# A gated mix of a long convolution and a GEGLU block on one core: loads from two queues, last rows in four groups, a half tile of the down product in row halves, part of the final mix on ScalarE and GpSimd

## The chip, the core and the metric

The kernel runs on one core of a Trainium2 chip. A core has TensorE (PE in the profile; its weight loads are PEld), VectorE (DVE), ScalarE (ACT), GpSimd (POOL) and SyncE (SP), and 16 DMA engines that move data between DRAM and the on-chip memory. SP issues DMAs in order from its queue, and so can ACT from its own. Matrix products land in eight accumulation banks that DVE and ACT must empty ("evacuate") before they can be used again. The metric is the device time of one execution in microseconds (us), as the median of several; a lower time is better.

## The reference

The input is a sequence `x` of 2048 positions with 640 channels. The output mixes two branches with one gate value for each position:

```python
g = sigmoid((x * gate_w).sum(-1, keepdims=True))
a = conv(x, K) + x * Dskip          # K[d, l] = Re(sum_n C[d,n] * exp(dt*A[d,n]*l) * dt*B[d,n]), by FFT
b = (gelu(x @ w_gate) * (x @ w_up)) @ w_down
return g * a + (1 - g) * b
```

The convolution is causal and as long as the sequence; its kernel `K` is made from complex parameters `A`, `B`, `C` with 128 states for each channel. The inner width of `b` is 1728, that is 13 tiles of 128 and one half tile of 64.

## The kernel before

**The work.** The convolution is a product of spectra. The transforms are matrix products with sine tables, in two stages: stage A works across 16 "phases" (positions modulo 16) and its result goes through a DRAM buffer (`dU` for the input, `dKA` for the kernel K) so that stage B finds other rows together. K itself is built for half of the channels at a time (`kgen`, L736): exponentials on ACT (L647, L675), phases on DVE (L624 to L628), sines on ACT (L633), their products on DVE (L661, L662, L685), a contraction with 640 small matmuls for both halves (L711), a selection (L722), a store to `dS` (L731), and 18 gathers out of `dS` (L804, L812) that feed stage A (L840). A spectrum and its copy with swapped rows (L881) are multiplied with K's spectrum (L888). The inverse stage B (L899) works in eight chunks `c`; each chunk is evacuated by ACT or DVE (L259, L263) and stored to `dY` (L907). `finish` (L910) loads from `dY` into eight tiles (L913), does the last stage with `WAT` for 16 phases (L922) and mixes each phase on DVE (L927): `z = psum * g + z`, where `z` already holds `(1 - g) * b`. Two stores for each pair of phases bring it out (L931).

**The block b.** For two halves of the sequence, `gate` (L536) and `up` (L557) multiply into pairs of banks; ACT applies gelu (L548), DVE multiplies (L568). The last weight tile holds the 64 gate columns and the 64 up columns side by side, so for tile 13 the up half is read from the upper 64 rows of the bank (L552). `downs` (L584) makes 16 tiles of the down product, each from 28 matmuls: 14 tiles of the inner width (tile 13 with zeros in its lower half, set by GpSimd at L486 and L531) times two column halves.

**The order of the work.** Every step is an entry of a `Plan`: which engines may do it, what it reads and writes, a cost and a rank. A planner's result, the list `ORDER` (952 numbers), is written into the kernel: each number names a step, its engine and its bank pair, and `emit` (L130) issues the steps in exactly this order. The costs (`mm`, `dma`, the numbers in `ve(...)`, `pool(...)`) therefore issue nothing; they are the planner's input only. Each engine works through its own steps in the order of the list. All DMAs are issued by SP, one after the other, and a DMA that waits holds those behind it.

**Names used later.** `ldtT` is log_dt, `prT` the parameters A to C, `xT` four transposed tiles of x (640 KB each), `Wg`, `Wu` and `Wd` weight tiles, `un` and `ua` one phase of x and its stage A, `kst` and `kst2` the contraction's results, `last_rows` (L400) the one-column fields from which `WAT`'s phases (L949 to L952) are made, `z` or `zt` the output tiles.

Of the kernel before, what the change touches and what calls it, by code (L numbers as in the profile page):

```python
# [27 lines left out]
    12 336 6316 316 536 436 516 396 1432 24 376 692 676 988 416 496 476 456 356 616 1004 576 636 1564 556 44 1628  # L28
    656 736 936 596 1064 816 756 2740 1608 64 956 776 716 836 876 1104 1588 796 916 1044 976 2861 1024 896 2836 84
    856 1648 1664 2982 2956 2768 1084 4383 1724 3076 3008 104 2780 2888 1164 1688 4404 1124 1442 1501 2856 2903 1144  # L30
    2804 1748 1784 2976 3020 2924 128 3096 1208 1464 6323 9384 6362 1496 1524 6436 1704 3341 1556 4428 1188 1228
    6388 6348 3436 3222 3044 3368 6416 1764 3103 3316 3248 1808 3380 3196 4444 1844 6441 3456 3262 6468 3404 1868
    1824 6481 3336 3700 6556 6508 3128 6536 1244 3461 3796 3284 3728 144 3143 3556 3488 1884 1268 6562 3216 6600
    3581 6676 6588 6628 1284 168 6656 1304 3822 3676 1324 1344 3608 3500 3916 3848 6721 3576 6748 6682 6796 1364
    6708 4181 3524 6776 1388 3164 3942 4276 4208 1404 2124 6840 4036 6803 3968 3861 6916 6868 2184 6828 2008 3622
    6896 3936 1904 3740 3696 2088 2024 3884 1928 6963 3816 3764 6921 6988 7036 2104 2048 3980 3644 6948 2064 1968
    4063 7016 1944 4056 4004 2148 4222 1984 4156 184 7081 264 4296 7040 2208 7156 2244 7108 7068 4301 2224 288 7136
    208 4088 224 4376 4244 7200 4328 7163 7224 4102 7276 7188 4344 248 7256 2164 4176 4124 2268 7280 2304 7323 4501
    7396 7348 7308 2284 7376 2328 2364 4702 4528 9484 2388 7443 7400 2344 4661 7516 7428 7468 2404 9508 7496 9544
    4728 2420 4688 9604 7523 2444 7562 7548 2461 7636 7588 7616 2503 2484 7640 2524 7682 7668 2541 7756 7708 4580  # L40
    2564 9408 7736 7803 9468 4604 7762 4461 7876 7784 7824 9524 9448 7856 2580 2622 9788 4743 4484 2644 9428 9804
    2604 9828 2716 7881 4764 7922 2676 4620 7996 7904 7948 2736 2696 9844 9908 7976 9748 9924 8556 4543 4644 9868
    8436 8376 9764 8236 8456 9568 9884 8576 8516 8536 8416 8256 8041 4564 8476 8002 4900 8496 8024 8116 8068 8316
    9664 9628 8296 8096 5023 8396 4996 8336 9584 8276 4928 8356 4782 5116 5048 9644 8121 4876 4808 8160 5063 8148
    8188 9688 9944 8216 5382 5136 5141 5476 5084 9968 9704 8620 5236 8583 8608 8648 4823 10064 5408 8676 4940 4896
    5168 4844 10004 8682 5016 8721 8708 5423 8748 8776 4964 10028 5182 5496 5444 9984 5261 5256 5204 10088 8820
    10124 5356 8783 5742 8808 8848 5503 5288 10184 5836 8876 5620 5768 5596 9724 11236 5528 11016 10044 8921 5648
    5716 5302 8948 10104 10148 8883 5324 5376 5540 8904 8976 5781 5564 5616 10208 10164 11322 11283 5856 11020 11348
    11304 11048 8982 5804 9023 9008 5660 9048 10224 9076 11142 11456 10241 5684 11168 5736 11243 11362 10264 10360
    11268 11388 9083 10384 9121 9108 11582 9144 11460 11608 11103 11484 11061 9176 11128 11542 11676 11564 11500  # L50
    11088 10323 12116 11524 9182 10344 9221 9208 10280 9248 9276 11682 11803 10304 11656 11721 11708 11416 11748
    11216 12242 11824 11196 12200 12268 12121 11636 12224 9283 11436 12148 9322 11896 9304 9348 10400 10441 10424
    9376 12163 11762 10468 12184 6080 11788 10536 10496 11856 10516 11876 5861 6108 12316 12296 10556 5983 5956 5888
    12616 12756 6122 6008 6076 11900 11941 6144 11983 11928 11968 12020 12004 5902 12476 12048 12336 13176 13216
    13256 13236 6161 5924 13336 13436 13196 13376 5976 12663 12620 6188 6242 12684 13296 13516 12644 13416 13356
    12724 13276 12343 13496 12481 6268 12704 12520 12096 13316 12364 12508 13396 13456 6284 12548 12383 6201 13476
    12408 12896 12584 13036 12076 12424 13620 12444 13522 13648 13563 13544 13588 12800 12828 12564 13723 13616
    13662 13748 6224 12760 14556 13688 12943 12964 12788 13081 13716 13042 13108 13064 12900 13763 14336 12928 13821
    13124 13862 13788 6020 12984 13888 13816 13144 13848 13004 13916 13963 10892 14642 6044 13921 13988 13948 14683
    14664 14560 14708 14601 14016 14584 14916 14462 14628 14343 14776 14484 14368 14020 14061 14048 10904 14123  # L60
    14382 14148 14084 14160 14188 14263 14404 14116 14221 14288 15180 14216 14244 14962 14756 15208 15263 14736
    14984 14921 15288 14316 15500 14944 14422 15528 10643 14444 10928 12844 14536 14516 12864 10952 15004 14781
# [978 lines left out]
```

## Time and profile before

| quantity | value |
|---|---|
| median of 3 runs | 312.56 us (311.97 to 314.31) |
| profiled execution: time, span | 310.86 us, 309.1 us |
| PE busy | 260.2 us (84%), 2446 matmuls |
| PEld busy | 142.4 us (46%) |
| DVE busy | 246.8 us (80%), 373 instructions |
| ACT busy | 221.8 us (72%), 274 instructions |
| POOL busy | 5.2 us (2%), 17 instructions |
| DMA | 60.62 MB, queue busy 60.6% of 16 engines |
| chain that ended last | PE 41%, DVE 12%, DMA 11%, SP's queue 8%, ACT 5% of the span |

The span runs from the first to the last recorded instruction of one profiled execution; the execution's own time has a little more around it. A busy share is an average over the whole span, and the stages have different limits. PE's busy time is modelled: matmuls overlap, so a busy PE is not PE at its peak. A group's row gives its line, engine, operation, the form (partitions x elements, type), the count, the busy time, the mean time of one in ns, and the engine's idle time ahead of it with what ended most of that. Instructions of one engine overlap a little, so the distance between two starts can be less than the mean duration. The chain of waits is followed back from the last instruction; "issue" in it is time in which the engine waited for nothing that the profile shows, and SPq is the DMA issue on SP's queue.

### The profile page before, as it was taken

The numbers are of one execution on the slowest core, as the hardware profiler recorded it, in microseconds if no ns is written. First come the engines' busy times: TensorE is split into PE (matmuls) and PEld (weight loads), VectorE is DVE, ScalarE is ACT, GpSimd is POOL, SyncE is SP. The second block draws the span as 40 slices with busy tenths as digits, with TensorE's granted clock in tenths as the row PEclk, the third lists the DMA queues.
The fourth block names the chain that finished last, engine by engine and source line by source line (L and its number), as shares of the span: only waits on it lengthen the run. The fifth ranks groups of instructions, "written<-read, shape, count | busy, mean of one in ns | idle before, by whom it ended". The sixth has DMA issues, their size and how long they took to land.

```text
span 309.1 us, 6162 instructions
## 1 busy us (share of the span) xinstructions
PE 260.2 (84%) x2446; PEld 142.4 (46%) x2446; DVE 246.8 (80%) x373; ACT 221.8 (72%) x274; POOL 5.2 (2%) x17
## 2 busy tenths in 40 slices
PE   0699899899599799997899986998677999999471
PEld 0253344344257676743444455443233656666230
DVE  4999999999999849689999874526768799993494
ACT  3999999999998689999898952853558845640000
POOL 4000000000000000000000000000001100000000
PEclk9999999999799999999999997799959999999975
DMA  6995344444231321645336567996597976789886
GB/s 205 391 296 168 106 140 133 127 127 129 85 127 67 108 78 54 186 139 155 106 113 200 200 194 257 334 348 193 168 335 272 333 220 193 279 266 343 254 245 171
DMA packets 45859, 60.62 MB, mean 196 GB/s; under 512 B 4803, under 2 KB 38150, under 8 KB 45830
## 3 DMA queue, kind: packets, MB, share of 16 engines
q1 hardware_dynamic: 45830, 60.23, 60.6%
q8 instruction: 19, 0.31, 0.4%
q14 instruction: 10, 0.08, 0.1%
HBM read 35.80 MB, written 19.17 MB: 178 GB/s over the span
## 4 chain that ended last, share of the span: by engine, by line
PE 41%; DVE 12%; DMA 11%; SPq 8%; ACT 5%; issue 4%; DVEq 0%; ACTq 0%
PE ps L592 12%; PE ps L544 10%; PE ps L564 8%; SPq L804 4%; DMA arena<-dU 4%; ACT arena L259 3%; PE ps L711 3%; DMA dY<-arena 3%; DVE arena L685 3%; DVE arena L927 3%; DVE arena L568 2%; PE ps L867 2%; PE ps L899 2%; SPq L913 2%; DVE arena L263 2%
## 5 line engine op out<-in xcount | busy, mean ns | idle before, releaser
L259 ACT CAST arena<-ps 128x640 bf16<-128x640 f32 (+1 forms) x110 | 70.5, 696 | 34.9 <-PE ps L867 11.0
L544 PE MATMUL ps<-arena 128*128 128x512 bf16 x280 | 67.0, 397 | 15.8 <-DMA arena<-in_w_gu_dram 11.0
L592 PE MATMUL ps<-arena 128*128 128x320 bf16 x448 | 63.2, 299 | 0.0
L564 PE MATMUL ps<-arena 128*128 128x512 bf16 x260 | 60.4, 384 | 2.1 <-ACT arena L259 0.8
L263 DVE CAST arena<-ps 128x640 bf16<-128x640 f32 (+3 forms) x62 | 50.4, 847 | 14.5 <-PE ps L711 6.9
L544 PEld LDWEIGHTS <-arena 128*128 128x128 bf16 x280 | 28.1, 101 | 51.5 <-issue 11.5
L592 PEld LDWEIGHTS <-arena 128*128 128x128 bf16 x448 | 43.0, 98 | 18.2 <-issue 0.8
L633 ACT ACTIVATE arena<-arena 128x2560 bf16<-128x2560 int16 x18 | 41.6, 2334 | 1.3 <-DVE arena L628 0.9
L568 DVE TENSOR_TENSOR arena<-ps,arena 128x1024 bf16<-128x1024 f32 x26 | 31.5, 1219 | 13.2 <-PE ps L564 13.1
L564 PEld LDWEIGHTS <-arena 128*128 128x128 bf16 x260 | 25.4, 99 | 32.4 <-issue 4.4
L548 ACT ACTIVATE arena<-ps 128x1024 bf16<-128x1024 f32 (+1 forms) x28 | 27.2, 1022 | 8.8 <-PE ps L544 8.5
L888 DVE TENSOR_TENSOR arena<-arena 128x1280 bf16<-128x1280 bf16 x32 | 24.5, 818 | 2.2 <-DMA arena<-arena 1.9
L867 PE MATMUL ps<-arena 64*64 64x320 bf16 x256 | 18.1, 334 | 7.0 <-DMA arena<-dKA 1.8
L647 ACT ACTIVATE arena<-arena 128x640 bf16<-128x640 f32 x32 | 21.0, 745 | 1.3 <-DVE arena L737 1.2
L265 DVE TENSOR_SCALAR arena<-ps,omg 128x640 bf16<-128x640 f32 x10 | 8.8, 881 | 11.0 <-PE ps L592 11.0
L626 DVE SCALAR_TENSOR_TENSOR arena<-arena 128x320 int32<-128x320 f32 x40 | 16.9, 484 | 0.0
L867 PEld LDWEIGHTS <-arena 64*64 64x64 bf16 x256 | 8.7, 110 | 16.9 <-issue 10.7
L675 ACT ACTIVATE arena<-arena 128x320 bf16<-128x320 f32 x40 | 16.3, 511 | 0.0
L927 DVE SCALAR_TENSOR_TENSOR arena<-ps,g_f,arena 128x640 bf16<-128x640 f32 x16 | 13.1, 877 | 3.6 <-PE ps L922 3.5
L711 PE MATMUL ps<-arena 128*64 128x40 bf16 x640 | 12.3, 189 | 4.2 <-issue 3.7
L840 PE MATMUL ps<-arena 128*128 128x320 bf16 x64 | 13.0, 326 | 3.1 <-DMA arena<-dS 2.1
L628 DVE TENSOR_SCALAR arena<-arena 128x1280 int32<-128x1280 int32 x18 | 14.9, 827 | 0.6
(105 smaller groups left out, 227.9 us busy)
## 6 DMA issues: line engine op xcount, KB each, us to landing
arena<-in_w_gu_dram SPq DMA_DIRECT2D x52, 160.0 KB, 2.3
dU<-arena SPq DMA_DIRECT2D x16, 320.0 KB, 2.3
dKA<-arena SPq DMA_DIRECT2D x16, 320.0 KB, 4.0
arena<-dU SPq DMA_DIRECT2D x8, 640.0 KB, 4.7
arena<-arena SPq DMA_DIRECT2D x16, 320.0 KB, 3.6
arena<-dKA SPq DMA_DIRECT2D x16, 320.0 KB, 4.0
dY<-arena SPq DMA_DIRECT2D x8, 640.0 KB, 5.5
arena<-in_u_nat_dram SPq DMA_DIRECT2D x16, 160.0 KB, 2.3
```

Source lines behind the costliest of these rows:

```text
L259: nc.scalar.copy(out=dst, in_=src(b))
L263: nc.vector.tensor_copy(out=dst, in_=src(b))
L544: nc.tensor.matmul(ps[:, k + j, :], lhsT=Wg[w][:, kt, :], rhs=xT[2 * grp + j][:, kt, :], start=(kt == 0), stop=(kt == NKT - 1))
L548: add({"ACT": an(1024) + 60}, lambda s: nc.scalar.activation(out=HTall[0:p, :, f, :], in_=ps[0:p, plan.bank(g):plan.bank(g) + 2, :], func= ...
L564: nc.tensor.matmul(ps[:, k + j, :], lhsT=Wu[w][:, kt, :], rhs=xT[2 * grp + j][:, kt, :], start=(kt == 0), stop=(kt == NKT - 1))
L568: add({"DVE": v1(1024)}, lambda s: nc.vector.tensor_tensor(out=HTall[:, :, f, :], in0=ps[:, plan.bank(u):plan.bank(u) + 2, :], in1=HTall[: ...
L592: nc.tensor.matmul(ps[:, k + h, 0:W], lhsT=HTq[q][:, f, 128 * j:128 * j + 128], rhs=Wd[f][:, W * h:W * h + W], start=(f == 0), stop=(f == ...
L633: ac(an(8 * W) + 90, lambda: nc.scalar.activation(out=t[:], in_=ph.bitcast(I16)[:, :, :, 0:16:2], func=ACT.Sin, scale=SIN_SCALE), r=[f"ph{ ...
L711: nc.tensor.matmul(ps[64 * y:64 * y + 64, k + i // g, 40 * (i % g):40 * (i % g) + 40], lhsT=cs1[:, x, 80 * y + k0 + i, :], rhs=cs2[:, x, 8 ...
L867: nc.tensor.matmul(ps[64 * y:64 * y + 64, k + x, 0:W], lhsT=TB[64 * x:64 * x + 64, m, :], rhs=t[64 * x:64 * x + 64, 2 * a + y, HV[h]], sta ...
L888: ve(v2(W * CS), lambda x=x: nc.vector.tensor_tensor(out=x[:, :, HV[h]], in0=x[:, :, HV[h]], in1=t, op=ALU.mult), r=ks, w=[k for k in kx i ...
L927: add({"DVE": v1(D)}, lambda s, p=p, ph=ph, z=z: nc.vector.scalar_tensor_tensor(out=z, in0=ps[:, plan.bank(p):plan.bank(p) + 2, 0:W], scal ...
```

## The change

- `dma` gets an argument `q`, the queues from which a transfer may be issued; ACT's queue is allowed for some. In the new list ACT issues the loads of log_dt, A_re and A_im, two loads of the last rows and six of the 16 output stores. All others stay on SP.
- The eight chunks of `dY` are put into four groups of rows in place of three (chunks 0 to 3, 4 and 5, 6, 7), and a load of the last rows covers one, two or four tiles in place of one: 12 loads in place of 24. `last_rows` is changed to fit the new row order and moves from DVE to GpSimd, where it is 18 one-column instructions.
- The half tile 13 is copied by a DMA from the lower to the upper 64 rows (`HTall[0:FL]` to `HTall[FL:128]`), its weights are loaded into both row halves, and the two memsets go. In `downs` the last matmul of each column half uses 64 rows, one half each.
- In the final mix, phases 1, 4, 7 and 10 go another way: ACT writes `psum * g` in fp32 to one of three buffers, and GpSimd adds it to `z`.
- The planner's costs are changed (for example `mm` from n / 2.28 + 4 to n / 2.36 + 4), and `ORDER` is new as a whole (945 numbers).

```diff
-    def dma(kb, fn, r=(), w=(), rank=5.0, run=1280, **k):
-        return add({"SP": 450}, lambda s: fn(), r, w, rank=rank, lat=1900, x=max(100, kb * (3.7 if run < 1000 else 3.3 if run < 2500 else 2.9)), **k)
+    def dma(kb, fn, r=(), w=(), rank=5.0, run=1280, q=("SP",), **k):
+        def go(s):
+            queue[0] = nc.scalar if s["eng"] == "ACT" else nc.sync
+            fn()
+
+        return add({e: 450 for e in q}, go, r, w, rank=rank, lat=1900, x=max(100, kb * (3.3 if run < 1000 else 2.8 if run < 2500 else 2.7)), **k)
...
     def last_rows():
...
+        v = nc.gpsimd
+        s_, hi, lo = sc8[:, 6:7], sc8[:, 9:10], sc8[:, 10:11]
+        x, y = sc8[:, 12:13], sc8[:, 14:15]
+        v.tensor_scalar(out=x, in0=B2, scalar1=4.0, scalar2=P5, op0=ALU.mult, op1=ALU.add)
...
+        for out, p7, p1, p0 in ((s_, x, y, P3), (hi, B4, B3, B2), (lo, B3, B2, B1)):
+            select(v, y, B1, p7, p1, 13)
+            select(v, out, B0, y, p0, 13)
...
-    ve(2000, last_rows, r=["fld"], w=["lrow"], rank=P["T2"])
+    pool(5000, last_rows, r=["fld"], w=["lrow"], rank=P["T2"])
...
+    dma(160, lambda: queue[0].dma_start(out=ldtT[:], in_=A_log_dt.partition_broadcast(N)), w=["ldtT"], rank=0, q=("ACT",))
...
+        dma(80, lambda: queue[0].dma_start(out=Wd[NFF][FL:128, :], in_=B_w_down[128 * NFF:128 * NFF + FL, :]), w=[(f"Wd{NFF}", 1)], rank=rank)
...
+            dma(128, lambda: queue[0].dma_start(out=HTall[FL:128, :, f, :], in_=HTall[0:FL, :, f, :]), r=HK(f), w=[(f"HT{q}", "z") for q in range(2)],
+                rank=RMUL, run=640)
...
                 for h in range(2):
-                    for f in range(NFT):
+                    for f in range(NFF):
                         nc.tensor.matmul(ps[:, k + h, 0:W], lhsT=HTq[q][:, f, 128 * j:128 * j + 128], rhs=Wd[f][:, W * h:W * h + W],
-                                         start=(f == 0), stop=(f == NFT - 1))
...
+                                         start=(f == 0), stop=False)
+                for h in range(2):
+                    nc.tensor.matmul(ps[:, k + h, 0:W], lhsT=HTq[q][FL * h:FL * h + FL, NFF, 128 * j:128 * j + 128],
+                                     rhs=Wd[NFF][FL * h:FL * h + FL, W * h:W * h + W], start=False, stop=True)
...
-        for q, (p0, st, cs) in enumerate(((0, 2, (0, 1, 2, 3)), (1, 4, (4, 5)), (3, 4, (6, 7)))):
-            for g, (t, nm) in enumerate(tiles):
...
+        rows = ((0, 2, (0, 1, 2, 3), (2, 2, 2, 2)), (1, 4, (4, 5), (4, 4)), (3, 8, (6,), (4, 4)), (7, 8, (7,), (1, 1, 2, 4)))
+        for q, (p0, st, cs, gs) in enumerate(rows):
+            g = 0
+            for n in gs:
+                dst = wide[g // 4][p0:128:st, 4 * (g % 4):4 * (g % 4 + n), :]
...
+                    q=("SP", "ACT") if q == 3 else ("SP",))
+                g += n
...
+                if ph not in POOLED:
+                    add({"DVE": 880}, lambda s, p=p, ph=ph, z=z: nc.vector.scalar_tensor_tensor(
+                        out=z, in0=ps[:, plan.bank(p):plan.bank(p) + 2, 0:W], scalar=g_f[:, ph:ph + 1], in1=z, op0=ALU.mult, op1=ALU.add),
+                        r=["g"], w=[(f"zt{ph // 8}", ph % 8)], frees=p, rank=R)
+                    continue
+                y, yn = tmp[POOLED.index(ph) % len(tmp)]
+                add({"ACT": 800}, lambda s, p=p, ph=ph, y=y: nc.scalar.activation(
+                    out=y.rearrange("p (h w) -> p h w", h=2), in_=ps[:, plan.bank(p):plan.bank(p) + 2, 0:W], func=ACT.Copy, scale=g_f[:, ph:ph + 1]),
+                    r=["g"], w=[yn], frees=p, rank=R)
+                pool(1700, lambda ph=ph, y=y: nc.gpsimd.tensor_tensor(
+                    out=zt[ph // 8][:, ph % 8, :], in0=y, in1=zt[ph // 8][:, ph % 8, :], op=ALU.add), r=[yn], w=[(f"zt{ph // 8}", ph % 8)], rank=R)
...
+                    r=[(f"zt{g // 4}", 2 * (g % 4) + b) for b in range(2)], rank=R, run=2560, q=("SP", "ACT"))
```

In the new list, the order of the steps that the prediction speaks of is this. SP begins with one `un`, xT0, Wg0, xT1, the second half of the last down weight tile and Wg1. The four stores to the second half's `dS` are adjacent on SP, and between its first and last gather stand nine other transfers: a store to `dKA`, two row swaps, four loads of K chunks, a weight load and the second copy of half tile 13. After the last inverse matmuls PE does three down tiles (before: two), then the last rows of phases 13, 14, 9, 15, 12, 4, 3, 5, 1, 2, 7, 6, 0, 8, 10, 11. ACT does the mixes of phases 4, 1, 7 and 10 in this order with its output stores between them, and GpSimd its adds in the same order. The last output stores, of phases 10 and 11, are issued one on each queue.

## The prediction

> **What bounds the kernel now.** I read the page's totals first, then the busy time by stretch, then the end of the chain of waits with the timeline beside it, then groups and transfers. The profiled execution took 310.86 us (span 309.1 us, 1.76 us around it); the median of the three runs is 312.56 us, 1.7 us more. Busy time by stretch (length; busy us and instructions of PE, PEld, DVE, ACT, POOL; granted clock; DMA share; GB/s); 175.4 is the end of the last sine of the kernel generation, 282.9 the point where only two down products are left besides the last rows:
>
> ```profile
> 0.00:175.40 175.40, 153.09 (x1174) 80.95 (x1174) 154.95 (x260) 161.80 (x187) 3.13 (x15) 0.99 0.47 151
> 175.40:282.90 107.50, 94.20 (x1182) 54.31 (x1179) 77.05 (x96) 60.04 (x89) 2.09 (x2) 0.94 0.79 262
> 282.90:309.10 26.20, 12.91 (x96) 7.19 (x94) 14.84 (x18) 0.00 (x0) 0.00 (x0) 0.74 0.79 232
> ```
>
> So there are three limits. In the first stretch ACT is busy 161.8 of 175.4 us, DVE and PE close behind: a balance of three. In the second PE is busy 94.2 of 107.5 and DMA 79%. In the third ACT and POOL do nothing, and DVE works 14.8 of 26.2 us. From the timeline (start, length, engine, line, count, idle before):
>
> ```profile
> 279.41 7.78 PE L592 MATMUL ps<-arena 128*128 128x320 bf16 x56
> ...
> 284.28 10.02 SPq L913 DMA_DIRECT2D arena<-dY  x16
> ...
> 290.32 0.73 PE L922 MATMUL ps<-arena 128*64 128x320 bf16 x8 [3.13 <-DMA arena<-dY]
> 290.90 3.28 DVE L927 SCALAR_TENSOR_TENSOR arena<-ps,g_f,arena 128x640 bf16<-128x640 f32 x4 [2.79 <-PE ps L922]
> ...
> 294.39 11.56 SPq L931 DMA_DIRECT2D out_dram<-arena  x16
> 294.91 9.87 DVE L927 SCALAR_TENSOR_TENSOR arena<-ps,g_f,arena 128x640 bf16<-128x640 f32 x12 [0.73 <-PE ps L922]
> ```
>
> The last inverse ends on PE at 279.4. Two down tiles hide the way of its result through DRAM until 287.2; then PE idles 3.1 us. SP issues 16 loads at 0.6 us each, so the loads come one by one, and afterwards 16 mixes on DVE set the end. The chain says the same:
>
> ```profile
> 275.49 8.77 DMA dY<-arena
> ...
> 289.25 0.59 SPq L913
> 289.84 0.04 issue
> 289.88 3.13 DMA arena<-dY
> ```
>
> The rows for prices, by form (busy, mean ns), and DMA issues (us to landing):
>
> ```profile
> L592 PE MATMUL ps<-arena 128*128 128x320 bf16 x448 | 63.2, 299 | 0.0
> ...
> L927 DVE SCALAR_TENSOR_TENSOR arena<-ps,g_f,arena 128x640 bf16<-128x640 f32 x16 | 13.1, 877 | 3.6 <-PE ps L922 3.5
> ...
> L949 POOL IOTA arena<- 128x1024 int32 x2 | 2.1, 1044 | 238.3 <-PE ps L564 227.9 <-ACT arena L952 10.3
> ...
> L486 POOL MEMSET arena<- 64x640 bf16 x1 | 0.6, 626 | 0.0
> ```
>
> ```profile
> dY<-arena SPq DMA_DIRECT2D x8, 640.0 KB, 5.5
> ...
> arena<-dY SPq DMA_DIRECT2D x8, 320.0 KB, 4.7
> arena<-dY SPq DMA_DIRECT2D x16, 160.0 KB, 2.8
> ```
>
> **The change part by part.** Every instruction has a place in the order list, and the whole list is new, so I decoded both lists and counted what each engine does up to the same milestones.
>
> **Start.** Three loads (log_dt, A_re, A_im) go from SP to ACT's queue. SP issued log_dt third, at 1.66 us, and it released the first exponential at 5.38; on ACT it can go at 0.74, 0.9 us earlier. Against it: the 640 KB of xT0 now enter second on SP instead of seventh, and parameter loads issued later, beside such traffic, took 6.1 instead of 3.7 us, so the end of the range is a loss of 2.4. I take a gain of 0.5 (the log_dt load still has a lead of one issue). The three issues cost ACT nothing: it idled 3.4 us there. The extra 80 KB of the last weight tile stand ahead of Wg1 on SP (0.43 us of issue), which is not needed before the second gate.
>
> **To the last sine.** The counts differ by this. ACT: two table loads fewer (22 for 24; 2 x 1.28), 8 evacuations of the u transform fewer (8 x 0.65 between starts), two kst evacuations more (2 x 0.9): -6.0 us. DVE: those 8 (8 x 0.77 = +6.2), two kst fewer (2 x 1.1 = -2.2), the last-row fields gone to GpSimd (10.66 to 13.02: -2.4), two more fields of 0.07: +1.7. ACT comes to about 156, DVE to 156.7. If ACT went on binding with its old idle time the gain would be 6.0; if DVE binds, a loss of 1.7. Equal sums make the two wait for each other, so I take 1.5. On GpSimd the fields are 18 instructions of one column; the nearest row is its one-column IOTA at 0.135 (2.4 us in all), and even ten times that is hidden: GpSimd idles until its IOTA at about 235 us. The two copies of half tile 13 (128 KB, nearest row 2.3 to 2.8 us) precede a down tile by 15 or more entries. They cost nothing unless SP is held: first copy, SP holds the u loads behind it; second, see the third rival.
>
> **Down product.** 28 full matmuls become 26 and two half-row ones. Two tiles on end took 7.61 us (0.136 a matmul), a tile alone 3.90: leaving and returning to the 64x64 form costs about 0.1. If the halves overlap fully the tile gains 0.14; if the pair costs as much as two (0.27) plus 0.1 it loses 0.1. The nearest row is the lone group of four 64x64 matmuls, 0.26 (274.57 to 274.83) against 0.18 in a long row. So I take 0.07, 1.1 us for 16 tiles, bounds -1.6 to 2.2; on a path that PE alone sets lie the three tiles behind the last inverse, whose 0.2 is in the sum below, and I count the others at nothing, since ACT, DVE and SP cover them (without that cover, 0.9). "TensorEngine Tiling (Array Packing)" of the Trainium skill, section Key Properties, says that a change of tiling mode drains the engine; the trace's 0.08 to 0.1 is that size, and with two changes in every tile the page would leave no gain, 0.2 us less in the sum.
>
> **Second stretch.** Ahead of the second half's gathers stand stores to dS1. Their issues took 5.6 us (197.86 to 203.45), then K loads held SP until 208.71, and the 18 gathers with two others lasted to 221.84: 24.0 us. In the new list the four stores are adjacent (2 us), landing takes 3.6 (the row of these stores), then 27 issues of 0.6: about 21.8, 2 us less. Against it stand 9 foreign transfers among the gathers. I take 1.0; bounds: 5 gained (PE has 3.5 us less ahead of that contraction) to 3 lost.
>
> **From the last inverse to the last rows.** Three down tiles (was two) now follow it. PE: 3 x 3.83 = 11.5 us. Transfers: evacuation 1.1, store to landing 3.7 (280.53 to 284.28), three issues 1.8, landing of 640 KB about 5 (between the rows of 4.7 and 5.5): 11.6. The first last-row matmul therefore stands 11.6 us after the inverse, was 10.9, but with 3.8 us of work moved in there: 3.1 gained, and 2.7 taken. Were the landing 8.8 (the longest of a 640 KB transfer in the chain), 0.7 lost. What is late next is that landing and PE, about level.
>
> **The end.** Before, from the first last-row matmul: 18.8 us (290.32 to 309.10): 0.6, mixes 13.9, 4.3 from the last mix. After: DVE 12 x 0.82 = 9.8, and two queues take one issue (0.6) off the end: 0.6 + 9.8 + 3.7 = 14.1, a gain of 4.7. ACT's mixes cost 0.79 each (its scaled evacuation's row). A GpSimd add has no row: lower bound one write, 0.63; upper three passes at IOTA's 1.02 ns an element, 1.96; I take two, 1.3. Its chain: the second DVE mix frees a bank pair at 2.3, the last-row matmuls of phase 4 are done at 2.8, ACT's mix at 3.6, four adds later 8.8 (11.4 at the upper bound, 1.0 past DVE). On ACT the stores wait in order: behind the store that waits for add 4 are mixes 7 and 10, and for them GpSimd's last two adds; 4.9 + 0.5 + 0.8 = 6.2 is just when GpSimd has finished its second add, so nothing is lost there. So 4.4, range 2.5 to 5. "GPSIMD Engine Reference", Engine selection, advises VectorE for two-input work, GpSimd being about twice as slow; twice DVE's 0.88 would be an estimated 1.76, the chain 10.6, the sum 0.2 worse. No run here shows it.
>
> Sum: 0.5 + 1.5 + 1.0 + 2.7 + 4.4 = 10.1. 310.86 - 10.1 = 300.8; beside a median, 1.7 more: 302.5.
>
> **The rivals.** First, only the end gains: the balanced first 280 us give nothing (for it: three engines near 90%; against: ACT's 6 us). Then 312.56 - 2.7 - 4.4 = 305.5. Second, nothing changes: DVE binds the first stretch (+1.7), the start loses 1.0, the 640 KB landings take 8.8 (+0.7), and GpSimd's adds leave 2.5: about 313.5 (for it: DVE's sum is the larger one). Third, slower: SP is in order, and between the dS1 stores and the last gather it now has the tile-13 copy (waits for DVE), swaps (for evacuations) and K loads (for buffers). SP's longest waits are 6.3 and 5.5 us; three of 6.3, 18.9 less the 2 us of slack, delay the whole K chain: 302.5 + 16.9 = 319.4. It decides from 15 us of such waits on (302.5 + 13 is 1% over). Against it: in the list each producer stands well ahead.
>
> **How the numbers follow.** Forecast 0.60, first rival 0.24, second 0.09, third 0.07. 1% (3.1 us) is about what a measurement of this kernel can tell from no change. The forecast's own bounds, not all at once, are 295.5 to 308; the first rival's reach 310. The range 295.5 to 310 leaves out the last two rivals and little else. Faster 0.84, same 0.09, slower 0.07.
>
> **What would show it.** First exponential at 4.5 to 5.4 us; last sine near 173.5; last gather near 218; PE without a gap over 1 us between the last inverse and the last rows; 12 DVE mixes ending about 10.5 us after the first last-row matmul, and under 15 us from it to the end. Wrong if GpSimd's adds are over 2.5 us, the end of the chain is POOL, or the DVE idles more in the first stretch than before.

## The result, and the profile after

The changed kernel took 325.32 us (median of 4 runs, 322.36 to 328.29), the kernel before beside it 313.12 us (4 runs). The ratio is 1.0358, 95% interval 1.0255 to 1.046: slower, by 11 us, where 10 us less was predicted. The ratio leaves out the slowest execution of the changed kernel (328.29 us, at the lowest granted clock, 0.921), which was also the profiled one, so the lines of "after" below are those of the first experiment, the same kernel run again (execution 325.16 us, span 323.4 us). Single profiles differ by a few us; a cause is called shown only where the medians carry it.

Busy time by stretch, columns as before; 186.50 is the end of the last sine (before: 175.4), 293.20 the point where two down products are left. The fourth line runs to the end of the last inverse.

```profile
0.00:186.50 186.50, 157.96 (x1169) 82.01 (x1181) 157.75 (x258) 157.86 (x180) 8.07 (x31) 0.96 0.46 144
186.50:293.20 106.70, 92.18 (x1142) 50.44 (x1145) 72.31 (x89) 62.95 (x94) 2.09 (x2) 0.92 0.79 254
293.20:323.40 30.20, 15.38 (x122) 10.05 (x120) 12.34 (x15) 3.17 (x4) 5.60 (x4) 0.79 0.76 235
0.00:289.35 289.35, 246.29 (x2284) 129.90 (x2299) 229.05 (x345) 220.41 (x272) 10.17 (x33) 0.95 0.57 182
```

ACT's busy time in the first stretch fell from 161.8 to 157.9 us and DVE's rose from 155.0 to 157.8, close to the counts (156 and 156.7). Yet the stretch is 11.1 us longer: no engine is above 85% in it, where ACT was at 92%.

The timeline from the last inverse on (start, length, engine, line, count, idle before):

```profile
288.19 2.85 SPq L919 DMA_DIRECT2D dY<-arena  x3
...
289.35 3.71 PE L601 MATMUL ps<-arena 128*128 128x320 bf16 x26
...
296.13 5.01 SPq L930 DMA_DIRECT2D arena<-dY  x6
...
307.04 3.41 PE L941 MATMUL ps<-arena 128*64 128x320 bf16 x24 [5.98 <-DMA arena<-dY]
...
309.95 8.01 DVE L947 SCALAR_TENSOR_TENSOR arena<-ps,g_f,arena 128x640 bf16<-128x640 f32 x10 [0.46 <-PE ps L941]
...
310.86 8.31 SPq L958 DMA_DIRECT2D out_dram<-arena  x10
```

The chain of waits over the same time (start, length, what):

```profile
290.42 9.03 DMA dY<-arena
299.46 7.43 DMA arena<-dY
307.04 2.89 PE ps L941 x20
```

PE still idles, 5.98 us where it was 3.13, although a third down product now lies there. The store takes 9.03 us to land and the load 7.43. The DMA issues (count, KB each, median us to landing) show what the larger loads cost; the parameter loads are those of the start:

```profile
arena<-dY SPq DMA_DIRECT2D x6, 640.0 KB, 7.2
...
arena<-in_params_dram SPq DMA_DIRECT2D x4, 160.0 KB, 4.4
...
arena<-in_params_dram ACTq DMA_DIRECT2D x2, 160.0 KB, 7.8
```

Groups by form (count, busy, mean ns, idle before): full and half down matmuls, DVE's mixes, GpSimd's adds.

```profile
L601 PE MATMUL ps<-arena 128*128 128x320 bf16 x416 | 59.2, 299 | 0.6 <-ACT arena L264 0.3 <-DVE arena L268 0.2
...
L947 DVE SCALAR_TENSOR_TENSOR arena<-ps,g_f,arena 128x640 bf16<-128x640 f32 x12 | 9.7, 876 | 6.2 <-PE ps L941 6.2
L955 POOL TENSOR_TENSOR arena<-arena 128x640 bf16<-128x640 f32 x4 | 5.6, 1399 | 51.6 <-ACT arena L952 51.6
L604 PE MATMUL ps<-arena 64*128 64x320 bf16 x32 | 5.0, 306 | 0.0
```

### The profile page after: what moved, and what is told of

It is laid out like the page before. It is cut to its first block, busy times and chain, and to the rows that moved or that the text cites. A ratio compares the mean times of both kernels' runs of the same rounds, so it can differ in the third digit from the quotient of the medians.

```text
span 326.5 us, 6179 instructions
## 1 busy us (share of the span) xinstructions
PE 268.2 (82%) x2446; PEld 143.3 (44%) x2446; DVE 242.3 (74%) x361; ACT 223.9 (69%) x276; POOL 15.0 (5%) x37
## 4 chain that ended last, share of the span: by engine, by line
PE 54%; DMA 14%; ACT 11%; DVE 8%; SPq 7%; issue 3%; ACTq 0%; DVEq 0%
PE ps L573 15%; PE ps L601 12%; PE ps L551 11%; SPq L816 4%; ACT arena L264 4%; PE ps L723 4%; DMA arena<-in_params_dram 4%; PE ps L852 3%; DMA dY<-arena 3%; DVE arena L268 3%; PE ps L879 3%; ACT arena L687 2%; DMA arena<-dY 2%; DMA arena<-dU 2%; PE ps L788 2%
## 5 line engine op out<-in xcount | busy, mean ns | idle before, releaser
L264 ACT CAST arena<-ps 128x640 bf16<-128x640 f32 (+2 forms) x108 | 69.0, 698 | 33.9 <-PE ps L879 16.0
L551 PE MATMUL ps<-arena 128*128 128x512 bf16 x280 | 67.7, 396 | 19.3 <-DMA arena<-in_w_gu_dram 11.6
L268 DVE CAST arena<-ps 128x640 bf16<-128x640 f32 (+2 forms) x64 | 52.2, 849 | 24.1 <-PE ps L879 11.0
L573 PE MATMUL ps<-arena 128*128 128x512 bf16 x260 | 64.0, 402 | 3.6 <-ACT arena L264 3.1
L601 PE MATMUL ps<-arena 128*128 128x320 bf16 x416 | 59.2, 299 | 0.6 <-ACT arena L264 0.2
L551 PEld LDWEIGHTS <-arena 128*128 128x128 bf16 x280 | 27.6, 101 | 54.5 <-DMA arena<-in_w_gu_dram 13.0
L601 PEld LDWEIGHTS <-arena 128*128 128x128 bf16 x416 | 40.0, 98 | 17.7 <-issue 1.7
L573 PEld LDWEIGHTS <-arena 128*128 128x128 bf16 x260 | 26.5, 103 | 38.2 <-issue 13.0
L555 ACT ACTIVATE arena<-ps 128x1024 bf16<-128x1024 f32 (+1 forms) x28 | 27.6, 1023 | 11.6 <-PE ps L551 11.5
L879 PE MATMUL ps<-arena 64*64 64x320 bf16 x256 | 19.3, 337 | 8.8 <-DMA arena<-dKA 4.4
L952 ACT ACTIVATE arena<-ps,g_f 128x640 f32<-128x640 f32 x4 | 3.2, 794 | 24.1 <-PE ps L941 23.5
L270 DVE TENSOR_SCALAR arena<-ps,omg 128x640 bf16<-128x640 f32 x9 | 7.9, 882 | 12.4 <-PE ps L604 12.4
L879 PEld LDWEIGHTS <-arena 64*64 64x64 bf16 x256 | 7.7, 109 | 21.1 <-issue 11.8
L788 PE MATMUL ps<-arena 128*128 128x320 bf16 x64 | 12.2, 310 | 4.9 <-DMA arena<-in_u_nat_dram 4.2
L723 PE MATMUL ps<-arena 128*64 128x40 bf16 x640 | 13.1, 195 | 3.4 <-issue 3.2
```

The lines of the kernel that those rows point to most:

```text
L264: nc.scalar.copy(out=dst, in_=src(b))
L268: nc.vector.tensor_copy(out=dst, in_=src(b))
L551: nc.tensor.matmul(ps[:, k + j, :], lhsT=Wg[w][:, kt, :], rhs=xT[2 * grp + j][:, kt, :], start=(kt == 0), stop=(kt == NKT - 1))
L555: add({"ACT": an(1024) + 60}, lambda s: nc.scalar.activation(out=HTall[0:p, :, f, :], in_=ps[0:p, plan.bank(g):plan.bank(g) + 2, :], func= ...
L573: nc.tensor.matmul(ps[:, k + j, :], lhsT=Wu[w][:, kt, :], rhs=xT[2 * grp + j][:, kt, :], start=(kt == 0), stop=(kt == NKT - 1))
L601: nc.tensor.matmul(ps[:, k + h, 0:W], lhsT=HTq[q][:, f, 128 * j:128 * j + 128], rhs=Wd[f][:, W * h:W * h + W], start=(f == 0), stop=False)
```

## The experiments

Two theories stood against each other. In the first the edits cost the time, most likely the loads of the start on ACT's queue or the few large loads at the end. In the other the edits cost little and the new order list costs the time, by single waits (then one move mends it) or spread over the list. All kernels compute the whole result. Moves in the list are written with the names of the steps instead of their numbers; "gate 0.10" is the gate product of tile 10 for the first half of the sequence, "un15" the load of the last phase of x, "ev ua 4.1" the evacuation of the second part of phase 4's stage A, and "picks" are the selection products (L722 of the kernel before).

**Which part of the change?** First the changed kernel again; then all its edits under the old list; then only its three start loads put back; and the kernel before with nothing but the mixes and four output stores moved.

> The changed kernel once more, to have an undisturbed profile. Both theories: 321 to 325 us. Theory L (the new order list is at fault) expects the last sine of the kernel generation at 184 us or later (175.4 before) and gaps of PE over 2 us in the first 190 us that were not there before. Theory X (the edited instructions are at fault) expects the distance lost ahead of the last inverse to be small and most of it behind it.

325.82 us (321.73 to 327.75), ratio 1.0356 [1.0246, 1.0465].

```diff
-ORDER = the new list
+ORDER = the list of before up to the store of the fifth inverse chunk (its start loads on SP too), then the new tail
```

> All edits of the change, but the steps up to the store of the fifth inverse chunk in the order of before (the three start loads on SP again), then the change's own tail. Theory L: 313 us, within 3, because the first 260 us go as before and the tail gives nothing. Theory X: 320 us or more, since every edited instruction is still there.

313.57 us, ratio 1.0001 [0.9957, 1.0044]. With the same edits the old list gives the time of before. So the loss comes with the new list up to the fifth inverse chunk, the three start loads included (the next run takes these by themselves), and under the old list the edits gain nothing. The new list without the edits was not run. Busy time up to the end of the last inverse of this kernel, to be held against the fourth line above:

```profile
0.00:277.23 277.23, 237.69 (x2284) 127.89 (x2299) 225.97 (x341) 223.55 (x277) 9.45 (x33) 0.97 0.59 192
```

The same 2284 recorded matmuls take PE 8.6 us longer in the new list (246.29 against 237.69, at a granted clock of 0.95 against 0.97), and PE idles 3.5 us more (43.06 against 39.54). So in this pair of profiles most of PE's loss, as the profile models its busy time, is not idle time but matmuls that run slower. A lower clock is not the whole of it: of two executions at the same mean clock of 0.954, the one with the new list took 321.73 us and the one with the old list 313.83. The milestones of the two profiles part bit by bit: first exponentials begun +0.85, the table load that opens the second half's exponentials +3.9, last sine +9.5, last inverse +12.1, first last rows +13.5, end +13.3.

The waits up to the last sine (what waits, for what: us in total, times, longest), first with the new list:

```profile
DVE arena L577 <- PE ps L573: 11.3, 7, 4.2
...
PE ps L788 <- DMA arena<-in_u_nat_dram: 4.1, 1, 4.1
```

and with the old one, where the lines of the code stand four higher:

```profile
DVE arena L573 <- PE ps L569: 1.6, 3, 0.9
```

DVE, in order, stands behind products whose `up` matmuls are late, and PE behind a load of `un`; the old list has no PE wait of the second kind.

```diff
-ACT: load log_dt, load A_re, load A_im
+SP: load A_re; first un; load log_dt; xT0; Wg0; xT1; load A_im
```

> The changed kernel with the loads of log_dt, A_re and A_im on SP again, A_re and log_dt ahead of xT0. If the 2.4 us that the first exponential of the kernel generation comes later (9.8 for 7.4 us) reach the end: 319 to 322 us, 2 to 3 us faster than the changed kernel. If the list's other waits absorb them: no change, 323 us.

327.28 us, ratio 1.0461 [1.0377, 1.0546], with the first exponentials at 9.62 us. So ACT's queue for these three is not what costs the time: on SP, with the 640 KB of xT0 still early beside them, they come no sooner.

```diff
+POOLED = (1, 9, 10, 14): ACT writes psum * g, GpSimd adds it to z
+ACT: the last four output stores
```

> The kernel before with two parts of the change alone: four phases (1, 9, 10, 14) mixed by ACT and GpSimd, and four of the 16 output stores on ACT's queue; list and loads as before. The prediction's sum for the end gives 3 us less, between 1.5 and 4.5: 308 to 311 us. Theory X (GpSimd's adds slow DVE down, or end the chain): 313 us or more.

313.81 us, ratio 0.9992 [0.9946, 1.0039]. Four mixes off DVE and four stores off SP gain nothing that can be measured.

**Which half of the list?** One kernel takes the new list up to the first exponential of the second half and then the old one; the other the reverse.

```diff
+ORDER = new[:296] + what is left, in the old order
+ORDER = old[:299] + what is left, in the new order
```

> All edits of the change; the new order list as far as the first exponential of the kernel generation's second half (296 entries, about 116 us), from there the order list of before for what is left, and the changed tail. With the old list in both places this was 313.6 (ratio 1.000), with the new in both 325.8 (1.036). Theory A, the loss is made in the first 116 us (first exponentials 1.8 us later, the second half's first table load 5.7 us later than before): ratio 1.018 to 1.038, 319 to 326 us. Theory B, it is made behind that: ratio 0.995 to 1.010, 312 to 317 us. If each makes half, 319.

> The complement: the order list of before as far as the first exponential of the second half (299 entries, about 110 us), the new list behind that, all edits of the change. Theory A (loss in the first 116 us): ratio 0.995 to 1.010, 312 to 317 us. Theory B (loss behind it: PE's 4.1 us wait for the last u tile and ACT's waits of 3.8 and 3.0 us between 146 and 160): 1.018 to 1.038, 319 to 326 us.

327.88 us, 1.0461 [1.037, 1.0552], and 327.07 us, 1.0442 [1.0351, 1.0533]. Either half loses as much as the whole. What the seam itself costs can't be told apart, so this does not divide the loss; it only speaks against a single place.

**Is it the waits of PE?** On PE's timeline of the changed kernel two long waits stand out. The matmuls behind each run slower than the same work without a wait:

```profile
64.39 2.32 PE L551 MATMUL ps<-arena 128*128 128x512 bf16 x10 [0.74 <-DVE arena L268]
70.53 3.51 PE L551 MATMUL ps<-arena 128*128 128x512 bf16 x10 [3.82 <-ACT arena L264]
...
148.17 1.25 PE L788 MATMUL ps<-arena 128*128 128x320 bf16 x4 [4.12 <-DMA arena<-in_u_nat_dram]
149.21 8.72 PE L573 MATMUL ps<-arena 128*128 128x512 bf16 x29
```

Ten matmuls take 2.32 us, but 3.51 behind a wait of 3.82. The granted clock (last column but two) ahead of the second wait, behind it and later:

```profile
140.00:144.00 4.00, 4.00 (x19) 1.67 (x17) 3.97 (x6) 3.97 (x4) 0.00 (x0) 1.00 0.28 70
148.17:153.00 4.83, 4.83 (x13) 1.94 (x14) 1.31 (x3) 3.51 (x5) 0.00 (x0) 0.50 0.67 190
155.00:157.90 2.90, 2.90 (x15) 1.34 (x14) 2.02 (x5) 0.32 (x1) 0.00 (x0) 1.00 0.56 178
```

The first wait is for an evacuation that stands behind five groups of exponentials on ACT, the second for the last `un` tile (number 15), which the list puts behind twelve gathers on SP. The placement behind each was put into the old list, and mended in the new one.

```diff
 # old list, all edits:
-SP: 12 gathers; load un15; six gathers
+SP: all 18 gathers; load un15
 # old list, all edits:
-ACT: ev ua 5.1, ev ua 5.0 among the five groups of exponentials
+ACT: ev ua 5.1, ev ua 5.0 behind them
```

> The converse: all edits of the change with the old order list up to the tail (313.6 us, ratio 1.000), and in it the load of the last u tile moved behind all eighteen gathers. It went out at 137.1 us and PE used it at 139.9; now it goes out at about 142.5 and PE can use it at about 145. Theory S: PE waits 4 to 5 us, matmuls behind that are slower, 4 to 6 us more in all, ratio 1.013 to 1.020. Theory N: under 1.5 us, ratio 0.999 to 1.005.

> The other converse: the old list up to the tail, with two evacuations of the u transform (71.5 and 73.7 us on ACT) moved behind the five exponential groups of the first half, as the new list has it; nothing else is moved. Theory S: the gate product that needs their bank starts 2 to 3 us later, 1.5 to 3 us more, ratio 1.005 to 1.010. Theory N: PE's wait of 3.52 us at 82.4 takes it up, ratio 0.997 to 1.003.

The late tile: 317.13 us, 1.0136 [1.007, 1.0201]; PE's timeline has the wait and the slow matmuls behind it:

```profile
131.72 6.64 PE L547 MATMUL ps<-arena 128*128 128x512 bf16 x30
143.12 1.25 PE L784 MATMUL ps<-arena 128*128 128x320 bf16 x4 [4.77 <-DMA arena<-in_u_nat_dram]
144.16 4.13 PE L569 MATMUL ps<-arena 128*128 128x512 bf16 x10
```

So this wait of 4.8 us cost some 4 us. Ten matmuls of that form lost 1.8 us behind it (4.13 against 2.32). The Trainium skill has this as "TensorE: Matmul & The Clock Gate", Part 1: after an idle window of about 3.4 us the clock falls to half and returns after about as long of steady work. The matmuls behind the waits of 3.82, 4.12 and 4.77 us, and the clock of 0.50 above, agree with that.

Exponentials in a row: 314.01 us, 1.0033 [0.9991, 1.0075]. But PE's timeline has no long wait there, only two short ones:

```profile
75.23 2.32 PE L547 MATMUL ps<-arena 128*128 128x512 bf16 x10 [1.30 <-ACT arena L260]
...
82.27 2.10 PE L547 MATMUL ps<-arena 128*128 128x512 bf16 x9 [2.02 <-ACT arena L260]
```

In the old list without this move the second is 3.52 us and the first does not exist. So this run says that the placement is harmless in the old list; what the wait of 3.82 us costs in the new one it does not say.

```diff
 # new list:
-SP: nine gathers; load un15
+SP: load un15; nine gathers
 # and also, in the next kernel:
-ACT: five groups of exponentials; ev ua 4.1        PE: gate 0.10 ahead of up 0.6
+ACT: two groups of exponentials; ev ua 4.1         PE, DVE: up 0.6 and its product ahead of gate 0.10
 # and also, in the third:
-SP: nine gathers; store dU 14
+SP: store dU 14; nine gathers
 # and also, in the fourth: the 18 gathers of the second half adjacent, the nine other transfers behind them
```

> The changed kernel with one entry of the list moved: the load of the last u tile goes ahead of nine of the gathers that stand before it on SP. In the changed kernel it is issued at 145.65 and PE waits 4.12 us for it at 148.17; the 29 matmuls behind that wait take 8.72 us instead of 6.64, and ACT waits 3.81 and 2.97 us. Theory S (this wait on SP's queue is a real part of the 11 us): the wait is gone, 4 to 6 us less, ratio 1.016 to 1.024, 319 to 321 us. Theory N (something else is as late: the gathers, which now land later, or ACT): under 1.5 us less, ratio 1.031 or more.

> As the run with the last u tile ahead, and in the first half an evacuation of the u transform taken out from behind the five exponential groups that ACT runs in a row from 62 to 70 us, with the up product 0.6 ahead of the gate product 0.10 on PE. In the changed kernel PE waits 3.82 us there and its next 20 matmuls take 6.4 us instead of 4.5. Theory S: PE has 2 to 4 us more work done at 77 us; 1.5 to 4 us less than the run with the last u tile ahead, ratio 1.006 to 1.018. Theory N (ACT is the limit in this stretch and has no less to do): no difference from that run, within 1 us.

> As the run with the u tile and the evacuation (322.5 us, ratio 1.028), and the store of the u transform's phase 14 also goes ahead of the gathers. In the run with the u tile alone PE's wait was gone, but the next evacuation waited 3.36 us for that store, which then stood behind nine gathers on SP. Theory S: SP's order is what holds this place, so that wait goes too: 1.5 to 3.5 us less, ratio 1.016 to 1.024. Theory N: the gathers, now later, hold the K transform instead, within 1 us, 1.025 to 1.031.

> As the run before in this list, and the eighteen gathers of the second half follow each other on SP; the eleven other transfers that stand among them (copy of tile 13, swaps, K loads, a weight, a store) come behind. In the changed kernel the first of these gathers goes out 26.4 us behind the last sine (32.4 with the old list) but the last one 46.4 us behind it (46.05 with the old). Theory G, the last gather leads the second stretch: it goes out 6 to 8 us sooner, 2 to 5 us less, ratio 1.005 to 1.018. Theory K, the K loads and swaps behind it lead as much: within 1.5 us, or slower.

324.48 us, 1.0294 [1.0235, 1.0353]; 322.54 us, 1.0278 [1.0238, 1.0318]; 325.98 us (320.15 to 326.79: too wide for a ratio); 329.1 us, 1.0476 [1.0406, 1.0546]. The two moves together win back 2 to 3 us of 11, less than one of them cost in the old list. With un15 ahead, ACT stood at the next item of the same queue, the store of dU 14:

```profile
150.26 1.29 ACT L260 CAST arena<-ps 128x640 bf16<-128x640 f32 x2 [3.36 <-DMA dU<-arena]
```

With that ahead too (third kernel), PE stood at the gathers:

```profile
156.91 0.70 PE L848 MATMUL ps<-arena 128*128 128x320 bf16 x4 [3.62 <-DMA arena<-dS]
```

And with the second half's gathers in a row (fourth), at the loads of K that they had pushed back (PE's waits):

```profile
PE ps L875 <- DMA arena<-dKA: 8.4, 4, 6.2
```

Each mended wait is followed by the next, for something as late.

**Is it the chain of the first K?** In the new list the contraction of the first half starts at 111.9 us (old list 103.2), the stores to `dS` at 131.1 (124.7) and the gathers at 137.1 (128.3). If this lateness is what all those waits have in common, putting the chain first should bring most of the time back, and making it late in the old list should cost it.

```diff
 # new list with the first two moves:
+DVE: the last products of the first half ahead of a phase of the second    PE: contraction ahead of one more down product
+PE, DVE, SP: picks and dS stores right behind it    SP: gathers spread among the un loads, un14 and un15 ahead
 # old list, all edits:
+PE: contraction and picks behind two more down products and one phase of u; stores to dS and the exponentials of the second half behind it
```

> Theory H: what leads from about 95 us on is the kernel generation's first half. In the changed kernel its last sine ends at 105.5 us (100.9 with the old list and the same edits), its contraction starts at 111.9 (103.2), its stores to dS0 at 131.1 (124.7), the first gather at 137.1 (128.3), the first K transform on PE at 157.8 (149.5), the last inverse at 289.4 (277.2). This run is the one with the u tile and the evacuation (322.5 us, ratio 1.028) with that chain put first: the last two phase products on VectorE ahead of a phase of the second half, the contraction one down tile earlier, its pick products and stores right behind it, the gathers spread over the u loads. Theory H: contraction at 106 to 108 us, first gather before 125, no wait for u tiles, gathers or their stores between 120 and 160; 3 to 6 us less than that run, ratio 1.009 to 1.018. Theory N (the order of this chain is not what leads): within 1.5 us of that run, 1.023 or more.

> The converse: all edits with the old list up to the tail (313.6 us, ratio 1.000), and in it the contraction of the first half, its evacuations, pick products and stores stand behind two more down tiles and a u phase; the exponentials of the second half, which write where the contraction reads, come behind it. Theory H: contraction ends at 117 to 119 us (111.7 there), first exponential of the second half 5 to 7 us later, 5 to 8 us more in all, ratio 1.016 to 1.026. Theory N: the other engines take it up, under 2 us, ratio 1.006 or less.

326.11 us, 1.0405 [1.034, 1.047], slower than the kernel it starts from (322.54, 1.0278), though the contraction starts at 106.0, the stores at 120.0 and the gathers at 125.75, the last two ahead of the old list. ACT's timeline has the next wait, for DVE:

```profile
141.20 1.28 ACT L551 ACT_TABLE_LOAD   x1 [4.47 <-DVE arena L266]
```

So putting this chain first does not bring the time back; its lateness alone is not the cause. The late contraction in the old list took 328.52 us, 1.0482 [1.0423, 1.0542], but by another way than the changed kernel: the second half's exponentials write where the contraction still reads, and ACT stands still on that:

```profile
128.58 7.83 ACT L655 ACTIVATE arena<-arena 128x640 bf16<-128x640 f32 x12 [17.12 <-PE ps L719]
```

The changed kernel has no such wait, so this run says how dear the place is, not what the new list lost.

**Why does the end gain nothing?** With the old list and the new tail, three stretches of the end (columns as above; the DMA share is the last but one) show the transfers in two bursts:

```profile
286.00:294.00 8.00, 3.40 (x26) 2.23 (x26) 0.88 (x1) 0.00 (x0) 0.00 (x0) 0.94 0.90 259
294.00:298.00 4.00, 3.39 (x31) 2.58 (x27) 3.23 (x4) 0.80 (x1) 0.26 (x1) 0.69 0.02 4
298.00:308.00 10.00, 3.49 (x36) 1.89 (x31) 6.46 (x9) 2.38 (x3) 5.33 (x4) 0.94 0.83 252
```

Until 294 the loads land (share 0.90) and no mix can start; then the DMA engines stand empty (0.02) until the first stores, which fill them again. If finer loads let mixing start before the last has landed, the gap should close. Four forms were tried: 12 finer loads, eight of them on ACT's queue, with last rows, mixes and stores in the order of the groups; the mix-only kernel with eight of its last 16 loads there; the first form with all loads on SP; and this with all 16 mixes on DVE and every other output store on ACT's queue.

```diff
-        rows = ((0, 2, (0, 1, 2, 3), (2, 2, 2, 2)), (1, 4, (4, 5), (4, 4)), (3, 8, (6,), (4, 4)), (7, 8, (7,), (1, 1, 2, 4)))
+        rows = ((0, 2, (0, 1, 2, 3), (2, 2, 2, 2)), (1, 4, (4, 5), (2, 2, 2, 2)), (3, 8, (6,), (2, 2, 2, 2)), (7, 8, (7,), (2, 2, 2, 2)))
 # last form:
-    POOLED = (1, 4, 7, 10)
+    POOLED = ()
```

> The version with the old order list and the changed tail (313.6 us, ratio 1.000), but the loads behind the last inverse in twelve pieces of two groups (320 or 160 KB instead of up to 640), half of them on ACT's queue, last rows, mixes and stores in order of the groups. Theory D, the transfers set the end and the changed tail loses what it gains because no transfer can run between the landing of the last big load and the first store (4.5 us with a DMA share of 0.02 in that version): first last-row matmul at 11.5 to 13 us behind the last inverse instead of 16.3, the gap gone, ratio 0.980 to 0.990, 307 to 310 us. Theory M, the mixes and adds set the end: first last-row matmul earlier by the same, and the whole earlier by it too, 0.985, but the time from there to the end stays at 16.6 us; under D it grows to 18 us or more. Theory Q, each load's own way dominates: fins wait for loads one by one, ratio 0.998 to 1.005.

> Before, with four mixes on ScalarE and GpSimd and late output stores on ACT's queue (ratio 0.999), and with every other one of the last sixteen loads on ACT's queue too, all ahead of the mixes. Theory I, SP's 0.6 us an issue is what spaces the loads (16 in 10.0 us): issues done 5 us sooner, 309.5 to 311.5 us, ratio 0.987 to 0.994. Theory D, the transfers themselves (DMA share 0.75 to 1.0 from 276 to 303 us, 2.56 MB of loads and 2.56 MB of stores at 250 GB/s): no change, ratio 0.996 to 1.004.

> The run with twelve finer loads on two queues (315.3 us, ratio 1.005), with all twelve on SP's queue. There the first last-row matmul came at 11.8 us behind the last inverse as expected, but ScalarE's first mix then waited for the landing of its own queue's last load, PE 3.72 us for it, and no transfer ran from 293.5 to 297. Theory D (transfers set the end; that gap is what is lost): no such wait, first store near 291.5, 3.5 to 5.5 us less, ratio 0.984 to 0.994. Theory Q (the fins wait for loads one by one): 0.997 to 1.005.

> As the run with the finer loads on one queue, with all sixteen mixes on VectorE, and every other output store on ACT's queue: what the four mixes on ScalarE and GpSimd are worth once no load is late. Theory D: the transfers, not the mixes, set the end: within 1 us of that run. Theory M: four mixes more on VectorE, 3 us slower than that run.

In this order: 315.28 us, 1.0054 [1.0002, 1.0107]; 316.48, 1.0083 [1.0038, 1.0128]; 313.61, 0.9998 [0.9952, 1.0044]; 313.96, 0.9952 [0.9904, 1.0]. No form clearly beats the kernel before. The two with loads on ACT's queue are slower by a little. In them ACT's own first mix waits for the landing of those loads, and PE for ACT. PE's timeline of the first form, and ACT's of the second:

```profile
295.42 5.79 PE L938 MATMUL ps<-arena 128*64 128x320 bf16 x44 [3.72 <-ACT arena L949]
```

```profile
295.46 0.79 ACT L937 ACTIVATE arena<-ps,g_f 128x640 f32<-128x640 f32 x1 [15.96 <-DMA arena<-dY]
```

Nor does a second queue land each load sooner: in the second form the 160 KB loads took 4.3 us (ACT's queue) and 4.6 us (SP's), where 16 on SP alone had taken 3.1 (medians). The Trainium skill has what fits this in "DMA: Bandwidth & Descriptors", Queues, rings and completion order: the queues of SP and ACT are rings on the same 16 DMA engines. With all loads on SP, SP itself stood still among the output stores (its waits):

```profile
SPq L955 <- DMA out_dram<-arena: 5.7, 1, 5.7
```

And with all 16 mixes on DVE the end is no longer than with 12: the mixes do not set it. What does is left open between the landing of the loads and that of the stores.

## Why the prediction was wrong, point by point

The forecast put the span at 299.0 us; it was 323.4 in the profile of after. By segments the missing 24.4 us are 13.1 up to the last sine (173.4 implied, 186.5 measured), 3.6 from there to the last inverse (99.25, 102.85), 6.1 from there to the last rows (11.6, 17.7) and 2.3 at the end (14.1, 16.4), less 0.7 by which its terms were rounded down. The kernel with all edits under the old list divides this: by the two profiles 13.3 us belong to the list (9.5, 2.7, 1.4 and -0.2), and 11.8 are forecast gains that the edits under the old list do not show either.

- **The step that failed: "To the last sine".** Its counts were right to 2 us; what failed is "Equal sums make the two wait for each other, so I take 1.5". A sum of busy time bounds a stretch from below only. Its bounds, a gain of 6.0 and a loss of 1.7, were both such sums, so waits between engines were in neither. In place of 1.5 us gained, 11.1 were lost there, with ACT 4 us less busy. What came instead, by the two profiles up to the last inverse: PE 3.5 us more idle and 8.6 us slower in the same matmuls, and DVE 11.3 us behind late `up` products in the first stretch, where the old list has 1.6. That the loss comes with the list is shown; which placements cause it stays open. The moves and the chain put first settle only that mending none of the tried places brings most of it back.
- **The start** lost 1.8 us instead of gaining 0.5: the first exponentials began at 9.13 us (7.37 before). The log_dt load, meant to be 0.9 us earlier, released its exponential at 6.14 us (5.38 before), and the two parameter loads on ACT's queue landed after 7.8 us. The end of the range, 2.4 lost, was the nearer one.
- **The down product**: a tile followed by another takes 3.88 us (289.35 to 293.23), where it took 3.80 before (7.61 for two on end). So 0.08 is lost where 0.07 gained was taken. The two half matmuls take 0.24 to 0.31 where 0.27 would be two full ones, so the page that spoke of a drain at each change of tiling ("TensorEngine Tiling (Array Packing)", Key Properties), and so of no gain, was nearer than the sum.
- **The second stretch** gained 1.2 us in all, 3.8 of work moved out of it included. The first gather came 26.4 us after the last sine, the last 46.4 (46.05 with the old list): the list has nine foreign transfers among them, and the head start (26.4 us where the old list has 32.4) was gone at the last. From the first store to `dS1` to the last gather it took 27.4 us (205.46 to 232.88), where 24.0 were read before and 21.8 forecast. That is the third rival's mechanism in the place it named, at a price of nothing gained; its 18.9 us of waits did not come there. That rival's total, 319.4, was the nearest of the four, for another reason.
- **From the last inverse to the last rows** is the second term mis-sized: 17.7 us for 11.6. The store landed after 9.03 us where 3.7 were taken, the load after 7.43 where 5 were (7.75 and 7.33 under the old list, so this comes with the new tail). The 3.7 was a misreading: the load that went out at 284.28 had waited for the store before the last, whose 8.77 us stand in the chain shown before, and the last store itself took longer than 3.7 (kernel before, issued at 280.6):

```profile
dY<-arena SPq DMA_DIRECT2D x1, 640.0 KB, 5.3
```

With 8.77 in place of 3.7 the same sum gives 16.7 us. The prediction used 8.8 only as a bound for the load.
- **The end**: mixes and adds were priced well (0.876 and 1.399 us; 0.88 and 1.3 predicted). An add on GpSimd takes 1.6 times as long as a mix on DVE, which is another instruction; the estimate from "GPSIMD Engine Reference", Engine selection, was twice. But 16.4 us remain where 14.1 were forecast: "16 mixes on DVE set the end" was wrong. The kernel with only the mixes moved shows it (0.9992), and the one with all 16 on DVE again (0.9952).
- **Hidden work**: the last-row fields took GpSimd some 6.5 us in 18 instructions, nearly three times the 2.4 taken, and hid, as said.

Of the signs named beforehand, most spoke at once: the first exponential at 6.14 us instead of 5.4 at the latest, the last sine at 186.5 instead of 173.5, the last gather at 232.9 instead of 218, PE's gap of 5.98 us, 16.4 us at the end instead of under 15, and DVE idle for 28.8 us of the first stretch instead of 20.5.

## What to carry to other kernels

Where three engines are each about 87 to 92% busy, a new order for the whole kernel can't be priced by what each engine has to do: here counts right to about 1% left over 11 us open. So put a new order and the edits on the chip apart from each other. For a transfer that several others run beside, take the duration that it had in its own place in the trace, and see which transfer the next step really waited for. Before work is moved off an engine at the end, see whether the transfers around it stand empty or full: where they came in two full bursts, faster mixing was worth nothing here.

## What the runs showed of the hardware

A wait of 4 us on PE cost some 2 us more in the matmuls behind it: 29 of them behind a wait of 4.12 us took 8.72 us, where 30 of the same form took 6.64 without one, and the granted clock was 0.50 for the first 4.83 us. In the two profiles compared, up to the last inverse, slower matmuls (8.6 us) were more than the added idle time (3.5 us). Three 640 KB stores issued close together landed after 7.7, 8.8 and 5.3 us (kernel before); the medians of all eight were 4.4 to 6.2 in these runs. GpSimd's one-column instructions took 0.21 to 0.98 us each, up to seven times the 0.135 of the one-column IOTA of before.
